# Decode attention with a token mixer on one core: values one pair behind the scores, turns of the keys between the softmax steps

## The chip, the core and the metric

The kernel runs on one core of one Trainium2 chip. The engines that matter here are TensorE (PE, matmuls), VectorE (DVE), ScalarE (ACT), GpSimd (POOL) and SyncE (SP, which issues the DMAs). Each takes its instructions in the order of its own queue; an instruction that waits holds up all behind it. The metric is the device time of one execution in microseconds (us), as a median over runs, less is better.

## What is computed

One decode step for 8 sequences: x (8 tokens of 512 values) plus a grouped-query attention over a cache of 8192 positions, plus a small MLP over the token axis. All is float32. Cut to what matters:

```
x  = A_x;  xn = layernorm(x)
q  = xn @ wq                          # 32 query heads of 128
k, v: caches [B=8, Hkv=8, Sk=8192, Dh=128], four query heads share one key head
p  = softmax(q . k * Dh**-0.5)        # over the 8192 positions
o  = p . v
attention = o @ wo                    # [32*128, 512]
h  = layernorm(xn)
mixer = gelu(h * w1 + b1) . w2 + b2   # 1792 hidden units, one token position
out = x + attention + mixer
```

The keys and values of one (head, sequence) pair are 8192 x 128 floats each, 4 MB (4096 KB) for the keys and 4 MB for the values. There are 8 x 8 = 64 such pairs, and each cache entry is used for four queries only.

## The kernel before

The kernel goes through the 64 pairs i = 0 .. 63 (N_IT), head h = i // 8, sequence b = i % 8. Keys and values are loaded whole, one DMA of 4 MB each (128 partitions, 64 rows of 128 floats in each), into a ring of five buffers named raw (RING, line 36). The loads are listed in advance in `order` (lines 53 to 57: keys 0, values 0, keys 1, values 1, ..., with values 62 put behind keys 63), and `load_next` (67) issues the next one of the list on SP. A load takes the buffer that was taken five loads earlier, and waits on SP until its last reader is done. Three loads are issued ahead of everything, two more after the projection of q, then one in each `qk` and one in each `pv`. The very first keys come in four pieces, the last values in pieces of a half, a quarter and two eighths (line 74).

The steps of one pair:

- `turn(i, a)` (209): DVE transposes a quarter of the keys in place, in 32 x 32 blocks; four turns per pair.
- `qk(i)` (216): 16 matmul calls, 32 matmul instructions, give the scores S of the pair in one PSUM bank; then it issues a load.
- `sm_max` (230, DVE: maximum of a row), `sm_bias` (235: a matmul that spreads the maxima, and a DVE reduction over those of one query head), `sm_exp` (243, ACT: exponential and row sum), `sm_place` (251: a matmul that permutes rows, and a DVE transpose into PT).
- `pv(i)` (261): 16 calls, 32 instructions, multiply PT with the values; it can be called for a part (u0 to u1) of the rows; at its end it issues a load.
- `o_pick(i)` (275, three DVE instructions) takes the wanted blocks out of the product and adds them up; `o_place(i)` (284) adds the pair's columns to MH, a bank that collects one head.

Once a head: `o_sums` (292: row sums and their reciprocal), `o_scale` (299) and `o_project` (303: 32 matmul instructions with wo, then an addition to yacc on DVE), with wo of the head loaded by `load_wo` (83) into a single buffer at b = 2. The mixer of one token runs beside a head: `mx_begin` (315) at b = 0, two or three `mx_step` (324, ACT and POOL) in a pair, `mx_end` (331: 4 matmul calls and an addition). `q_place` (201) writes the queries of the next head into the weights W, at b = 3 to 6.

The schedule is manual: every engine executes in the order in which the code calls the steps. In the main loop (lines 359 to 390) that is, per pair: qk(i), the four softmax steps of i, turn(i + 1, 0), pv(i), mixer, turn(i + 1, quart), o_pick(i), turn(i + 1, 2 * quart), o_place(i), turn(i + 1, 3 * quart). At b = 7 come o_sums, mx_end, o_scale and o_project of the same head. The last two pairs are written out (392 to 416), and the result is stored from yacc (417).

Of the kernel before, what the change touches and what calls it, by code (L numbers as in the profile page):

```python
# [14 lines left out]
B, D, HQ, HKV, SK, DH, F = 8, 512, 32, 8, 8192, 128, 1792  # L15
REP = HQ // HKV
P = 128
NT = SK // P
# [9 lines left out]
N_IT = B * HKV  # L28
# [4 lines left out]
def attn_mixer_kernel(ctx: ExitStack, tc: tile.TileContext, x, kc, vc, wq, wo, w1, b1, w2, b2, out):  # L33
# [12 lines left out]
    def misc():  # L46
        return ps_m.tile([P, 512], F32, name="misc")
# [3 lines left out]
    KR, VR = {}, {}  # L51
    order = []
# [14 lines left out]
    def load_next():  # L67
        if order:
            _, src, to, i = order.pop()
            h, b = divmod(i, B)  # L70
            t = ring.tile([P, NT, DH], F32, name="raw")
            rows = src[b, h].rearrange("(p t) d -> p t d", p=P)
            at = 0
            for n in (NT // 4,) * 4 if to is KR and not i else (NT // 2, NT // 4, NT // 8, NT // 8) if not order else (NT,):
                nc.sync.dma_start(t[:, at:at + n, :], rows[:, at:at + n, :])
                at += n
            to[i] = t
            if not order:
                load_wo(HKV - 1)
# [3 lines left out]
    def load_wo(h):  # L83
        t = one.tile([P, REP, D], F32, name="wo")
        rows = wo[h * REP * DH:(h + 1) * REP * DH, :].rearrange("(r p) n -> p r n", p=P)
        if h < HKV - 1:
            for p in (slice(0, 8), slice(8, P)) if h == HKV - 2 else (slice(0, P),):
                nc.sync.dma_start(t[p], rows[p])
        else:
            for r in range(REP):  # L90
                nc.sync.dma_start(t[:, r, :], rows[:, r, :])
        wos[h] = t
# [116 lines left out]
    def turn(i, a, w=NT // 4):  # L209
        if i < N_IT:  # L210
            t = KR[i][:, a:a + w, :].rearrange("p t d -> p (t d)")
            nc.vector.transpose(t, t)  # L212
# [3 lines left out]
    def qk(i):  # L216
        h, b = divmod(i, B)
        S[i] = ps_s.tile([P, 512], F32, name="s")
        kt = KR.pop(i).rearrange("p (u g) d -> p g u d", g=NG)
        for j in range(NB):  # L220
            for g in range(NG):
                nc.tensor.matmul(S[i][g * Q:(g + 1) * Q, :], W[h % 2][:, b, j, :], kt[:, g, :, j * Q:(j + 1) * Q],  # L222
                                 start=(j == 0), stop=(j == NB - 1))
        load_next()
# [5 lines left out]
    def sm_max(i):  # L230
        mr = work.tile([P, 1], F32, name="mr")
        nc.vector.tensor_reduce(mr, S[i], AX.X, ALU.max)  # L232
        st[i] = mr

    def sm_bias(i):
        m = misc()
        nc.tensor.matmul(m[:, :P], st[i].to_broadcast([P, P]), ident, start=True, stop=True)  # L237
        t = one.tile([P, P], F32, name="sq")
        nb = work.tile([P, 1], F32, name="nb")
        nc.vector.tensor_tensor_reduce(t, m[:, :P], hmask, -SCALE, 3.0e38, ALU.add, ALU.min, nb)  # L240
        st[i] = nb

    def sm_exp(i):
        h, b = divmod(i, B)
        p = t2k.tile([P, 512], F32, name="t2k")
        nc.scalar.activation(p, S.pop(i), AF.Exp, bias=st[i], scale=SCALE, accum_out=LR[h % 2][:, b:b + 1])  # L246
        st[i] = p
# [3 lines left out]
    def sm_place(i):  # L251
        m = misc()
        nc.tensor.matmul(m, perm, st.pop(i), start=True, stop=True)  # L253
        PT[i] = work.tile([P, 512], F32, name="pt")
        nc.vector.transpose(PT[i], m)  # L255
# [5 lines left out]
    def pv(i, u0=0, u1=NU):  # L261
        if u0 == 0:
            O[i] = ps_o.tile([P, 512], F32, name="o")
        for u in range(u0, u1):
            c = u % NB
            nc.tensor.matmul(O[i][c * Q:(c + 1) * Q, :], PT[i][:, u * Q:(u + 1) * Q],  # L266
                             VR[i][:, u * NG:(u + 1) * NG, :].rearrange("p t d -> p (t d)"),
                             start=(u < NB), stop=(u >= NU - NB))
        if u1 == NU:
            del VR[i], PT[i]  # L270
            load_next()
# [3 lines left out]
    def o_pick(i):  # L275
        om = t2k.tile([P, 512], F32, name="t2k")
        nc.vector.tensor_tensor(om.rearrange("p (g d) -> p g d", g=NG), O.pop(i).rearrange("p (g d) -> p g d", g=NG),  # L277
                                dm.unsqueeze(2).to_broadcast([P, NG, DH]), ALU.mult)
        ob = work.tile([P, 256], F32, name="ob")
        nc.vector.tensor_add(ob, om[:, :256], om[:, 256:])  # L280
        nc.vector.tensor_add(ob[:, :DH], ob[:, :DH], ob[:, DH:])  # L281
        OB[i] = ob

    def o_place(i):
        h, b = divmod(i, B)
        if b == 0:
            MH[h] = ps_h.tile([P, 512], F32, name="mh")
        nc.tensor.matmul(MH[h][:, b * REP:(b + 1) * REP], OB.pop(i)[:, :DH], sel, start=True, stop=True)  # L288
# [3 lines left out]
    def o_sums(h):  # L292
        m = misc()
        for r in range(REP):
            nc.tensor.matmul(m[:, r * B:(r + 1) * B], sel[:, r:r + 1].to_broadcast([P, P]), LR[h % 2], start=True, stop=True)
        RD[h] = work.tile([P, REP, B], F32, name="rd")
        nc.vector.reciprocal(RD[h], m[:, :REP * B].rearrange("p (r b) -> p r b", r=REP))

    def o_scale(h):
        nc.vector.tensor_tensor(OTS[h % 2].rearrange("p r (b s) -> p r b s", s=BS)[:, :, :, 0],  # L300
                                MH.pop(h)[:, :REP * B].rearrange("p (b r) -> p r b", r=REP), RD.pop(h), ALU.mult)

    def o_project(h):
        m = misc()
        for r in range(REP):
            for j in range(NB):
                nc.tensor.matmul(m[j * Q:(j + 1) * Q, :D // NB], OTS[h % 2][:, r, :], wos[h][:, r, quarter[j]],
                                 start=(r == 0), stop=(r == REP - 1))
        nc.vector.tensor_add(yacc, m[:, :D // NB], yacc)
# [5 lines left out]
    def mx_begin(b):  # L315
        m = misc()
        nc.tensor.matmul(m, ident[:B, b:b + 1].to_broadcast([B, P]), hn, start=True, stop=True)
        hb = one.tile([P, D], F32, name="hb")
        nc.scalar.copy(hb, m)
        acc = one.tile([P, D], F32, name="macc")  # L320
        nc.gpsimd.memset(acc, 0.0)  # L321
        mx[b] = (hb, acc)

    def mx_step(b, j):
        hb, acc = mx[b]
        g = one.tile([P, D], F32, name="g")
        nc.scalar.activation(g, hb, AF.Gelu_apprx_tanh, bias=b1t[:, j:j + 1], scale=w1t[:, j:j + 1])  # L327
        nc.gpsimd.tensor_scalar(g, g, w2t[:, j:j + 1], 1.0, op0=ALU.mult, op1=ALU.mult)  # L328
        nc.gpsimd.tensor_add(acc, acc, g)  # L329

    def mx_end(b):
        m = misc()
        for j in range(NB):
            nc.tensor.matmul(m[j * Q:(j + 1) * Q, :D // NB], bsel[:, BO - BS * b:BO - BS * b + Q], mx[b][1][:, quarter[j]],  # L334
                             start=True, stop=True)
        nc.vector.tensor_add(yacc, m[:, :D // NB], yacc)
# [18 lines left out]
    quart = NT // 4  # L355

    for i in range(N_IT - 2):
        h, b = divmod(i, B)  # L360
        if i == 0:
            for a in range(4):
                turn(0, a * quart)
        qk(i)
        sm_max(i)
        sm_bias(i)
        sm_exp(i)
        sm_place(i)
        turn(i + 1, 0)
        pv(i)  # L370
        if b == 0:
            mx_begin(h)
        k = 2 if h + 1 < HKV else 3
        for j in range(k * b, min(k * b + k, NF)):
            mx_step(h, j)
        turn(i + 1, quart)
        o_pick(i)
        turn(i + 1, 2 * quart)
        o_place(i)
        if b == B - 1:  # L380
            o_sums(h)
            mx_end(h)
        if b == 2:
            load_wo(h) if h < HKV - 1 else None
        if 3 <= b < 3 + NB and h + 1 < HKV:
            q_place(h + 1, b - 3)
        turn(i + 1, 3 * quart)
        if b == B - 1:
            o_scale(h)
            o_project(h)  # L390

    h = HKV - 1
    i, e = N_IT - 2, N_IT - 1
    qk(i)
    sm_max(i)
    sm_bias(i)
    sm_exp(i)
    sm_place(i)
    for a in range(4):
        turn(e, a * quart)  # L400
    pv(i)
    qk(e)
    o_pick(i)
    sm_max(e)
    sm_bias(e)
    sm_exp(e)
    sm_place(e)
    o_place(i)
    o_sums(h)
    mx_end(h)  # L410
    for u0, u1 in ((0, 8), (8, 12), (12, 14), (14, 16)):
        pv(e, u0, u1)
    o_pick(e)
    o_place(e)
    o_scale(h)
    o_project(h)
    nc.sync.dma_start(out.rearrange("b s (j n) -> j (b s) n", j=NB), yacc[::BS, :])
# [27 lines left out]
```

## Time and profile before

| | |
|---|---|
| median of 3 runs | 1576.01 us (1573.36 to 1576.42) |
| the profiled execution | 1578.8 us, its span from first to last instruction 1576.9 us |
| mean granted TensorE clock | 0.736 of full speed |
| turn of a quarter of the keys (L212, DVE) | 2282 ns, 256 times |
| read from HBM | 553.69 MB |

The profile is of one execution. Its page gives busy times by engine, the span in 40 slices, the DMA queues, the chain of work that ended last (followed back from the last instruction, each step to what released it), and the costliest groups of instructions. L222 is line 222 of the code; PE is the matmul, PEld the load of its weights. In a group's row stand the busy time in us and the mean of one in ns, and after the second bar the engine's idle time just before these instructions and what ended most of it. A row of the table of stages gives, for one stretch of the span, the busy time of each engine with the number of instructions, then the granted clock of TensorE, the mean busy share of the 16 DMA engines, and GB/s. A row of DMA issues ends with the median time from issue to landing in us; a row of waits gives total us, times, and the longest.

### The profile page before, as it was taken

What the parts mean: (1) busy time and instruction counts of PE and PEld (TensorE: products, weight loads), DVE (VectorE), ACT (ScalarE), POOL (GpSimd) and SP (SyncE); (2) the same over time, 40 slices, a digit from 0 to 9 for tenths busy, and PEclk for the clock granted to TensorE, in tenths of its full rate; (3) what the DMA queues carried; (4) which work ended last, traced back from release to release, by engine and by line L of the source; (5) the groups of instructions that cost most, each with busy time, mean ns of one, the idle gap of its engine ahead of it and who ended that gap; (6) DMA issues with size and microseconds to landing.
All of it is one profiled execution on the core that took longest, in us unless ns stands there. A gap on an engine that the chain in (4) does not pass through costs nothing.

```text
span 1576.9 us, 12454 instructions
## 1 busy us (share of the span) xinstructions
PE 928.2 (59%) x5172; PEld 267.0 (17%) x5172; DVE 796.9 (51%) x835; ACT 289.0 (18%) x364; POOL 229.5 (15%) x244
## 2 busy tenths in 40 slices
PE   3565566565565555655656645665656655566556
PEld 3111112111121112111121111211112111121112
DVE  2554645544545546545455445445445455454454
ACT  0121111221121220221202211022211212112110
POOL 1020211211111101111201111011110211113100
PEclk9676677776777767776677776776768777776768
DMA  9999888998888988899889988899888998898880
GB/s 407 430 432 389 353 333 348 370 387 333 346 357 365 370 346 359 345 376 371 334 333 377 382 346 346 342 363 386 360 333 345 374 369 350 333 369 336 336 330 1
DMA packets 24099, 554.51 MB, mean 352 GB/s; under 512 B 2499, under 2 KB 2531, under 8 KB 6891
## 3 DMA queue, kind: packets, MB, share of 16 engines
q1 hardware_dynamic: 23899, 553.67, 86.4%
q8 instruction: 41, 0.67, 0.2%
q14 instruction: 15, 0.12, 0.0%
q0 software_dynamic: 128, 0.02, 0.0%
q10 hardware_dynamic: 16, 0.02, 0.0%
HBM read 553.69 MB, written 0.02 MB: 351 GB/s over the span
## 4 chain that ended last, share of the span: by engine, by line
PE 59%; issue 17%; DVE 15%; ACT 7%; DMA 1%; DVEq 0%; ACTq 0%; SPq 0%
PE o L266 24%; PE s L222 23%; PE misc L253 6%; ACT L246 4%; ACT t2k L246 3%; DVE pt L255 3%; DVE mr L232 3%; DVE t2k L277 3%; DVE raw L212 2%; PE misc L237 2%; DVE ob L280 2%; DMA raw<-in_A_wq_dram 1%; PE mh L288 1%; DVE ob L281 1%; DVE sq L240 1%
## 5 line engine op out<-in xcount | busy, mean ns | idle before, releaser
L212 DVE STREAM_TRANSPOSE raw<-raw 128x2048 f32<-128x2048 f32 x256 | 577.1, 2282 | 0.3
L222 PE MATMUL s<-raw,w 128*32 128x512 f32 x2048 | 359.3, 864 | 254.0 <-issue 221.8
L266 PE MATMUL o<-raw,pt 128*32 128x512 f32 x2048 | 370.3, 890 | 51.0 <-DVE pt L255 51.0
L328 POOL TENSOR_SCALAR g<-g,w2t 128x512 f32<-128x512 f32 x112 | 77.7, 694 | 1071.9 <-ACT g L327 1071.9
L232 DVE TENSOR_REDUCE mr<-s 128x1 f32<-128x512 f32 x64 | 44.3, 691 | 363.4 <-PE s L222 363.4
L246 ACT ACT_TABLE_LOAD x55 | 70.6, 1283 | 799.7 <-DVE nb L240 799.6
L253 PE MATMUL misc<-t2k,perm 128*128 128x512 f32 x128 | 96.2, 840 | 147.5 <-ACT t2k L246 147.5
L222 PEld LDWEIGHTS s<-raw,w 128*32 128x32 f32 x2048 | 90.0, 152 | 466.7 <-issue 433.7
L255 DVE STREAM_TRANSPOSE pt<-misc 128x512 f32<-128x512 f32 x64 | 45.9, 717 | 217.4 <-PE misc L253 217.4
L329 POOL TENSOR_TENSOR macc<-macc,g 128x512 f32<-128x512 f32 x112 | 142.7, 1274 | 9.3
L266 PEld LDWEIGHTS o<-raw,pt 128*32 128x32 f32 x2048 | 82.1, 155 | 351.8 <-issue 227.3
L327 ACT ACTIVATE g<-hb,b1t,w1t 128x512 f32<-128x512 f32 x112 | 91.1, 813 | 127.4 <-POOL macc L329 126.7
L277 DVE TENSOR_TENSOR t2k<-o,dm 128x512 f32<-128x512 f32 x64 | 44.2, 691 | 100.8 <-PE o L266 100.8
L246 ACT ACTIVATE t2k<-s,nb 128x512 f32<-128x512 f32 x64 | 44.0, 687 | 243.6 <-DVE nb L240 243.1
L288 PE MATMUL mh<-sel,ob 128*128 128x4 f32 x128 | 24.5, 262 | 94.5 <-DVE ob L281 94.5
L327 ACT ACT_TABLE_LOAD x54 | 69.3, 1283 | 1.4
L237 PE MATMUL misc<-ident,mr 128*128 128x128 f32 x128 | 31.2, 326 | 52.0 <-DVE mr L232 52.0
L253 PEld LDWEIGHTS misc<-t2k,perm 128*128 128x128 f32 x128 | 21.8, 213 | 159.7 <-ACT t2k L246 159.7
L288 PEld LDWEIGHTS mh<-sel,ob 128*128 128x128 f32 x128 | 19.1, 188 | 154.5 <-DVE ob L281 154.1
L240 DVE CUSTOM_DVE_ANT_0 sq<-misc,hmask 128x128 f32<-128x128 f32 x64 | 18.6, 291 | 44.2 <-PE misc L237 44.2
L237 PEld LDWEIGHTS misc<-ident,mr 128*128 128x128 f32 x128 | 19.0, 187 | 115.9 <-DVE mr L232 115.9
L321 POOL MEMSET macc<- 128x512 f32 x8 | 4.2, 524 | 194.4 <-PE misc L334 194.4
(67 smaller groups left out, 198.2 us busy)
## 6 DMA issues: line engine op xcount, KB each, us to landing
raw<-in_A_v_cache_dram SPq DMA_DIRECT2D x63, 4096.0 KB, 12.8
raw<-in_A_k_cache_dram SPq DMA_DIRECT2D x63, 4096.0 KB, 12.3
raw<-in_A_wq_dram SPq DMA_DIRECT2D x2, 4096.0 KB, 17.1
wo<-in_A_wo_dram SPq DMA_DIRECT2D x6, 1024.0 KB, 14.7
raw<-in_A_k_cache_dram SPq DMA_DIRECT2D x4, 1024.0 KB, 25.4
raw<-in_A_v_cache_dram SPq DMA_DIRECT2D x1, 2048.0 KB
raw<-in_A_v_cache_dram SPq DMA_DIRECT2D x1, 1024.0 KB, 9.4
raw<-in_A_v_cache_dram SPq DMA_DIRECT2D x2, 512.0 KB
```

What stands on the lines that cost most here:

```text
L212: nc.vector.transpose(t, t)
L222: nc.tensor.matmul(S[i][g * Q:(g + 1) * Q, :], W[h % 2][:, b, j, :], kt[:, g, :, j * Q:(j + 1) * Q], start=(j == 0), stop=(j == NB - 1))
L232: nc.vector.tensor_reduce(mr, S[i], AX.X, ALU.max)
L237: nc.tensor.matmul(m[:, :P], st[i].to_broadcast([P, P]), ident, start=True, stop=True)
L246: nc.scalar.activation(p, S.pop(i), AF.Exp, bias=st[i], scale=SCALE, accum_out=LR[h % 2][:, b:b + 1])
L253: nc.tensor.matmul(m, perm, st.pop(i), start=True, stop=True)
L255: nc.vector.transpose(PT[i], m)
L266: nc.tensor.matmul(O[i][c * Q:(c + 1) * Q, :], PT[i][:, u * Q:(u + 1) * Q], VR[i][:, u * NG:(u + 1) * NG, :].rearrange("p t d -> p (t d)") ...
L277: nc.vector.tensor_tensor(om.rearrange("p (g d) -> p g d", g=NG), O.pop(i).rearrange("p (g d) -> p g d", g=NG), dm.unsqueeze(2).to_broadca ...
L327: nc.scalar.activation(g, hb, AF.Gelu_apprx_tanh, bias=b1t[:, j:j + 1], scale=w1t[:, j:j + 1])
L328: nc.gpsimd.tensor_scalar(g, g, w2t[:, j:j + 1], 1.0, op0=ALU.mult, op1=ALU.mult)
L329: nc.gpsimd.tensor_add(acc, acc, g)
```

## The change

The steps keep their code; their order changes. In a slot i, PE now does qk(i), then pv of the pair before, then the matmuls of sm_bias(i), o_place(i - 1) and sm_place(i). On DVE the turns of keys i + 1 stand between: turn 0, sm_max(i), turns 1 and 2, the reduction of sm_bias(i), o_pick(i - 1), turn 3, the transpose of sm_place(i). The calls of load_next stay in qk and pv, and so come in the order qk(i), pv(i - 1). o_sums, o_scale and o_project of a head stand in the first slot of the next one, mx_end at b = 7 (b = 6 in the last head), and the loop runs to pair 62, so that only the last pair is written out. The last keys are loaded in four pieces like the first ones. The number of instructions of each kind stays the same, save for the three DMAs that the pieces add.

```diff
--- before.py
+++ after.py
@@ -71,7 +71,7 @@
             t = ring.tile([P, NT, DH], F32, name="raw")
             rows = src[b, h].rearrange("(p t) d -> p t d", p=P)
             at = 0
-            for n in (NT // 4,) * 4 if to is KR and not i else (NT // 2, NT // 4, NT // 8, NT // 8) if not order else (NT,):
+            for n in (NT // 4,) * 4 if to is KR and i in (0, N_IT - 1) else (NT // 2, NT // 4, NT // 8, NT // 8) if not order else (NT,):
                 nc.sync.dma_start(t[:, at:at + n, :], rows[:, at:at + n, :])
                 at += n
             to[i] = t
@@ -356,62 +356,59 @@
 
 
 
-    for i in range(N_IT - 2):
+    LAST = N_IT - 1
+
+    def slot(i):
+
         h, b = divmod(i, B)
-        if i == 0:
-            for a in range(4):
-                turn(0, a * quart)
         qk(i)
+        turn(i + 1, 0)
         sm_max(i)
+        turn(i + 1, quart)
+        if i:
+            pv(i - 1)
+        turn(i + 1, 2 * quart)
         sm_bias(i)
+        if i:
+            o_pick(i - 1)
+            o_place(i - 1)
         sm_exp(i)
+        turn(i + 1, 3 * quart)
         sm_place(i)
-        turn(i + 1, 0)
-        pv(i)
         if b == 0:
             mx_begin(h)
+            if h:
+                o_sums(h - 1)
+                o_scale(h - 1)
+                o_project(h - 1)
         k = 2 if h + 1 < HKV else 3
         for j in range(k * b, min(k * b + k, NF)):
             mx_step(h, j)
-        turn(i + 1, quart)
-        o_pick(i)
-        turn(i + 1, 2 * quart)
-        o_place(i)
-        if b == B - 1:
-            o_sums(h)
-            mx_end(h)
-        if b == 2:
-            load_wo(h) if h < HKV - 1 else None
+        if b == 2 and h + 1 < HKV:
+            load_wo(h)
         if 3 <= b < 3 + NB and h + 1 < HKV:
             q_place(h + 1, b - 3)
-        turn(i + 1, 3 * quart)
-        if b == B - 1:
-            o_scale(h)
-            o_project(h)
-
+        if b == (B - 1 if h + 1 < HKV else B - 2):
+            mx_end(h)
+
+    for a in range(4):
+        turn(0, a * quart)
+    for i in range(LAST):
+        slot(i)
     h = HKV - 1
-    i, e = N_IT - 2, N_IT - 1
-    qk(i)
-    sm_max(i)
-    sm_bias(i)
-    sm_exp(i)
-    sm_place(i)
-    for a in range(4):
-        turn(e, a * quart)
-    pv(i)
-    qk(e)
-    o_pick(i)
-    sm_max(e)
-    sm_bias(e)
-    sm_exp(e)
-    sm_place(e)
-    o_place(i)
+    qk(LAST)
+    sm_max(LAST)
+    sm_bias(LAST)
+    sm_exp(LAST)
+    sm_place(LAST)
+    pv(LAST - 1)
+    o_pick(LAST - 1)
+    o_place(LAST - 1)
     o_sums(h)
-    mx_end(h)
     for u0, u1 in ((0, 8), (8, 12), (12, 14), (14, 16)):
-        pv(e, u0, u1)
-    o_pick(e)
-    o_place(e)
+        pv(LAST, u0, u1)
+    o_pick(LAST)
+    o_place(LAST)
     o_scale(h)
     o_project(h)
     nc.sync.dma_start(out.rearrange("b s (j n) -> j (b s) n", j=NB), yacc[::BS, :])
```

## The prediction

> **What bounds the kernel now.** I read the page's first lines and its chain of work first, then one pair of that chain, then the table of stages, then the DMA issues and the waits of SP's queue.
>
> ```profile
> span 1576.9 us, 12454 instructions
> PE 928.2 (59%) x5172; PEld 267.0 (17%) x5172; DVE 796.9 (51%) x835; ACT 289.0 (18%) x364; POOL 229.5 (15%) x244
> PE 59%; issue 17%; DVE 15%; ACT 7%; DMA 1%; DVEq 0%; ACTq 0%; SPq 0%
> ```
>
> No engine is busy for more than 59% of the span, and the chain that ended last consists of PE, DVE and ACT in turn, with 1% of DMA. So it is a serial chain, handed from engine to engine. One pair of it, in the view of the chain:
>
> ```profile
> 697.82 5.22 PE s L222 x32
> ...
> 703.81 0.50 PE misc L237 x2
> ...
> 708.25 0.73 DVE pt L255
> 708.98 0.04 issue
> 709.02 6.46 PE o L266 x32
> ...
> 717.41 4.43 issue
> 721.84 5.16 PE s L222 x32
> ```
>
> From scores to scores is 721.84 - 697.82 = 24.0 us: scores 5.2, softmax up to the values' start 6.0, values 6.5, then 6.3 in which DVE picks and still turns the second half of the next keys (shown as "issue"; DVE's turns lie there). Over the run 64 x 24.0 are 1536 of the 1576.9 us. Now the transfers.
>
> ```profile
> core 0: us, PE busy (x) PEld busy (x) DVE busy (x) ACT busy (x) POOL busy (x), PEclk, DMA share, GB/s
> 0.00:40.00 40.00, 15.53 (x292) 12.85 (x292) 10.70 (x39) 3.58 (x7) 5.32 (x13) 1.00 0.97 406
> 40.00:120.00 80.00, 44.81 (x212) 11.63 (x212) 43.49 (x42) 15.50 (x19) 11.81 (x12) 0.70 1.00 431
> ...
> 160.00:1540.00 1380.00, 821.95 (x4390) 228.40 (x4386) 709.99 (x716) 259.27 (x323) 207.97 (x215) 0.73 0.88 354
> ```
>
> ```profile
> DMA packets 24099, 554.51 MB, mean 352 GB/s; under 512 B 2499, under 2 KB 2531, under 8 KB 6891
> ...
> raw<-in_A_k_cache_dram SPq DMA_DIRECT2D x63, 4096.0 KB, 12.3
> ```
>
> ```profile
> 56.62 0.33 SPq L75 DMA_DIRECT2D raw<-in_A_v_cache_dram  x1
> ...
> 703.06 0.33 SPq L75 DMA_DIRECT2D raw<-in_A_v_cache_dram  x1
> ...
> 715.49 0.33 SPq L75 DMA_DIRECT2D raw<-in_A_k_cache_dram  x1
> ```
>
> ```profile
> SPq L75 <- PE o L266: 692.3, 61, 13.0
> ```
>
> While the transfers queued from the start lasted (40 to 120 us) the DMA engines were busy all the time and moved 431 GB/s, beside the same matmuls and turns as later. Afterwards SP waits for PE to free a buffer, and issues one tile at a time: the tile of 703.06 has landed some 12 us later, about when the next is issued at 715.49. The queue runs dry before each issue, and the rate drops to 354. So compute bounds the kernel, and the DMA floor lies close under it: one pair is 2 x 4.194 = 8.389 MB, at 431 GB/s **19.46 us**, against 24.0.
>
> **The change, part by part.** Values one pair later: pv(i-1) no longer waits for the softmax of its own pair; it follows qk(i) on PE, while DVE does the softmax and turns between its steps. What remains serial has to be compared with 19.46. The durations:
>
> ```profile
> L212 DVE STREAM_TRANSPOSE raw<-raw 128x2048 f32<-128x2048 f32 x256 | 577.1, 2282 | 0.3
> L222 PE MATMUL s<-raw,w 128*32 128x512 f32 x2048 | 359.3, 864 | 254.0 <-issue 221.8
> L266 PE MATMUL o<-raw,pt 128*32 128x512 f32 x2048 | 370.3, 890 | 51.0 <-DVE pt L255 51.0
> ...
> L232 DVE TENSOR_REDUCE mr<-s 128x1 f32<-128x512 f32 x64 | 44.3, 691 | 363.4 <-PE s L222 363.4
> ...
> L240 DVE CUSTOM_DVE_ANT_0 sq<-misc,hmask 128x128 f32<-128x128 f32 x64 | 18.6, 291 | 44.2 <-PE misc L237 44.2
> L277 DVE TENSOR_TENSOR t2k<-o,dm 128x512 f32<-128x512 f32 x64 | 44.2, 691 | 100.8 <-PE o L266 100.8
> ...
> L280 DVE TENSOR_TENSOR ob<-t2k 128x256 f32<-128x256 f32 x64 | 28.7, 449 | 2.2
> ...
> L281 DVE TENSOR_TENSOR ob<-ob 128x128 f32<-128x128 f32 x64 | 18.7, 292 | 2.2
> ```
>
> A turn is 2.28, scores 359.3/64 = 5.62, values 370.3/64 = 5.79, the pick 0.69 + 0.45 + 0.29 = 1.43. For the values behind the scores I keep two ends, since PE's clock changes within a burst:
>
> ```profile
> 722.67 0.23 PEld L222 LDWEIGHTS s<-raw,w 128*32 128x32 f32 x4 [0.62 <-issue]
> ...
> 725.49 0.14 PEld L222 LDWEIGHTS s<-raw,w 128*32 128x32 f32 x4 [0.29 <-issue]
> ```
>
> Four matmuls take 0.23 + 0.62 = 0.85 us early in the burst and 0.43 late in it, so 32 take 6.8 at the slow pace and 3.4 at the fast one: pv is 3.4 to 6.8. The Trainium skill ("TensorE: Matmul & The Clock Gate", Part 1) says that the clock is at half until about 3.4 us of activity have passed; the two rows agree with it. By that rule pv right behind qk is at the fast end: the sum below stays, and rival B loses ground.
>
> (1) The chain of one slot, with keys at hand: qk 5.62, pv 3.4 to 6.8, the bias matmul 0.5 (L237 in the chain), the reduction 0.37 with its read-out, the pick 1.43, the last turn 2.28, handovers 0.4: 14.0 to 17.4 us. Softmax's exp, placement and the turn of pt run beside pick and turn. DVE's own load is 796.9/64 = 12.5. All are below 19.46.
>
> (2) The loop through the buffers is the new risk. Five buffers are used in load order; qk(i) now issues the load of keys i+2, and that takes the buffer of values i-1, so it waits on SP for pv(i-1), and the load of values i+2 stands behind it in SP's queue. Both loads of a pair start together, after pv(i-1). Keys i+2 are needed in the next slot by turn(i+2, 0), which stands on DVE in front of sm_max(i+1): while it waits, the maximum, and with it the whole softmax, wait too. From the landing: turn 2.28, maximum 0.69, two turns 4.56, reduction 0.37, pick 1.43, turn 2.28, ten handovers of 0.05: 12.1 to the start of qk(i+2); then 5.62 and 3.4 to 6.8 to the end of pv(i+1), which frees the buffers again, two slots on. That is X = 21.1 to 24.5. With 12.3 from issue to landing on an empty queue the loop is 33.4 to 36.8 in two slots, 16.7 to 18.4 a pair. Below 19.46 again, by 2.1 to 5.5 us in two slots: the second tile of each pair keeps the queue filled until the next issue. So **the DMA becomes the bound** and streams.
>
> (3) Projection one pair later: removed from the end of a head, it now stands on PE between place(i) and the next scores at b = 0.
>
> ```profile
> L307 PE MATMUL misc<-wo,ot 128*32 128x128 f32 x256 | 14.6, 402 | 23.7 <-issue 23.4 <-DVE ot L300 0.3
> ...
> L317 PE MATMUL misc<-hn,ident 8*128 8x512 f32 x16 | 9.0, 639 | 0.0
> L295 PE MATMUL misc<-lr,sel 128*128 128x8 f32 x64 | 8.4, 257 | 0.0
> ```
>
> Per head that is 1.8 + 1.1 + 1.1, and about 0.5 of DVE between them, with handovers some 4.7 us seven times. Hidden by the margin of 5.5; at the other margin, 2.1, it costs 2.6 x 7 = 18 us. I take nothing and keep 18 for the range. The load of wo at b = 2 stays, one more MB in the stream; the mixer's steps and its end are beside it (ACT 18%, POOL 15%).
>
> (4) Last keys in four pieces: they land before DVE is free for them (below); worth nothing, and what cover fails is at most part of one transfer, some 7 us.
>
> **The sum.** By 40 us 40 x 0.406 = 16.2 MB have moved; 538.3 MB are left, at 431 GB/s 1249 us: the stream ends at S = 1289. In the start, scores 0 issue values 2 at 56.62 as now; the next issue comes with pv(0), after 8.4 of DVE (maximum, three turns, reduction), qk(1) and pv(0) itself, at 74 to 77. The eight tiles issued by then, 33.6 MB, last until 40 + 17.4/0.431 = 80: no gap. The end: behind keys 62 come keys 63, values 62, values 63 and 1 MB of wo, 13.6 MB or 31.6 us, so keys 62 land at S - 31.6, qk(62) starts 12.1 later at S - 19.5 and ends at S - 13.9, and after the maximum, three turns, reduction and pick (9.8) qk(63) starts at S - 4.1. The old end gives what follows:
>
> ```profile
> 1555.98 3.64 PE L222 MATMUL s<-raw,w 128*32 128x512 f32 x32 [3.48 <-issue]
> ...
> 1565.23 4.97 PE L266 MATMUL o<-raw,pt 128*32 128x512 f32 x32
> ```
>
> From 1555.98 to 1576.9 are 20.9; qk at its mean adds 2.0, values 62 and their pick, which had been done by then, 5.1 (the middle of 3.4 and 6.8) + 1.4. So 29.4 from S - 4.1: span 1289 + 25.3 = 1314. The profiled execution of before took 1578.8 for a span of 1576.9, so 1.9 more: 1316. The median of the runs, 1576.01, is 2.8 below it; in that proportion 1313.
>
> **Rivals.** (A) is this forecast; a rate half a per cent higher and a tail of 20 give 1302, and if the 406 of the first 40 us (with the start in it) were the rate, 1391; I take 431, the row with the same work beside it. **(B) The buffer loop decides.** If X is 28 rather than 24.5 the pair takes (12.3 + 28)/2 = 20.15, times 62 some 43 us more: 1356; at X = 30 it is 21.15 and 1418; at 31.7 the queue runs dry each slot by about what the issue costs, and it is 1470. For it: the margin is thin, handovers are estimates, PE's clock is uncertain. Against: even all matmuls at the slow pace (qk 6.8) leave X at 25.7. **(C) The memory gives no more than 354 GB/s for long**, and the 431 were a burst: then after 120 us, with 50.7 MB moved, the other 503.8 MB take 1423 us, and with the tail it is about 1567, 0.6% faster, give or take the tail. Against it: in the middle each tile is issued only when the one before has landed, so the empty queue explains the low rate. The Trainium skill ("DMA: Bandwidth & Descriptors", Specifications) gives about 358 GB/s as one core's limit on HBM; by that all 554.51 MB take 1549 us and the whole with its tail 1574, no change; the 80 us at 431 speak against it as a hard limit. **(D) Slower:** the turn at the head of DVE's queue. Were X above 2 x 24.0 - 12.3 = 35.7, a pair would take longer than 24. That wants 11 us more in X; its place would be the four turns, which now always run beside a transfer and beside matmuls that read the same buffers: from 5.1 us a turn on it decides, and at 5.5 a pair is 24.9 and the time about 1647. Against it, from 40 to 120 us, with the DMA always busy:
>
> ```profile
> L212 DVE STREAM_TRANSPOSE raw<-raw 128x2048 f32<-128x2048 f32 x16 | 35.8, 2278 | 0.0
> ```
>
> A turn took 2.28 there too. That the change would not do what it says has no case of its own: the orders of PE, DVE and SP are those of the code.
>
> **Chances and range.** A 0.70, B 0.20, C 0.05, D 0.05. The range, 1296 to 1375, holds A down to a rate of some 415 GB/s (1362) and the near part of B, up to X = 28.6. A change of 0.2% (3 us) is about what a measurement of this kernel can tell from none. A and B are faster; of C, whose time hangs on the tail and on the exact cap, I count 0.03 as faster and 0.02 as same; D is slower: faster 0.93, same 0.02, slower 0.05.
>
> **What would show it.** Right: in the middle stretch a DMA share near 1.00 and about 430 GB/s; issues of SP in pairs, one keys and one values at the end of L266; a time to landing some us above 12 for keys and above 22 for values; DVE waiting at L212 for a DMA; a pair of 19.5; PE's values at 3.4 to 6.8 directly behind the scores; the last transfers ending about 25 us before the end. B: a DMA share of 0.9 to 0.97, with L212 waiting and dips at b = 0. C: share 1.00 at a low rate. D: L212 far over 2.28. I would be wrong if a wait that I have not listed stands in DVE's queue, since everything there waits in line.

## The result, and the profile after

The changed kernel takes 1326.09 us (median of 4 runs, 1324.89 to 1326.68) against 1575.06 us for the kernel before (4 runs): ratio 0.842, 95% interval 0.840 to 0.843. The forecast was 1313 us with a range of 1296 to 1375. The profiled execution took 1324.89 us, its span 1323.1 us.

The page of the changed kernel: span, busy time, the DMA engines' share in 40 slices (tenths) with the rate below it, and the chain that ended last.

```profile
span 1323.1 us, 12383 instructions
PE 790.6 (60%) x5172; PEld 260.9 (20%) x5172; DVE 806.1 (61%) x835; ACT 289.0 (22%) x364; POOL 230.9 (17%) x244
...
DMA  9999999999999999999999999999999999999993
GB/s 397 437 432 427 429 427 434 432 427 429 432 430 430 427 432 431 431 424 432 432 431 427 429 430 427 434 422 429 432 429 428 433 342 429 435 430 420 432 423 126
...
DMA 53%; PE 22%; DVE 16%; issue 4%; ACT 4%; SPq 0%; ACTq 0%; DVEq 0%
```

The chain of before had 1% of DMA; this one has 53%. The engines do the same work (PE's busy time fell, since more of its matmuls ran at the fast pace), in 254 us less. The DMA digits are 9 from the first slice to the last but one. The table of stages of the changed kernel, columns as before:

```profile
40.00:120.00 80.00, 42.83 (x244) 11.97 (x244) 50.97 (x43) 15.90 (x20) 11.80 (x12) 0.72 1.00 429
...
160.00:1270.00 1110.00, 676.70 (x4256) 218.88 (x4260) 691.42 (x693) 256.38 (x319) 205.76 (x211) 0.75 1.00 427
...
1300.00:1324.00 24.00, 13.81 (x132) 5.17 (x124) 5.39 (x13) 0.78 (x2) 0.00 (x0) 0.93 0.05 20
```

The middle stretch, which had 0.88 and 354 GB/s, has 1.00 and 427. That is most of the gain: the 488 MB that took 1380 us at 354 GB/s take 1144 us at 427 GB/s, which is 236 of the 254 us. Groups of instructions, and below them the waits of SP's queue (total us, times, longest):

```profile
L212 DVE STREAM_TRANSPOSE raw<-raw 128x2048 f32<-128x2048 f32 x256 | 582.1, 2294 | 380.1 <-DMA raw<-in_A_k_cache_dram 380.1
L222 PE MATMUL s<-raw,w 128*32 128x512 f32 x2048 | 322.2, 785 | 17.0 <-issue 11.8
...
L266 PE MATMUL o<-raw,pt 128*32 128x512 f32 x2048 | 231.0, 592 | 0.0
```

```profile
SPq L75 <- DVE raw L212: 605.8, 62, 19.6
SPq L75 <- PE s L222: 393.3, 62, 12.0
SPq L75 <- PE o L266: 184.5, 61, 3.1
```

The wait has moved: DVE, which waited for no transfer before, waits 380.1 us at the first turn of a slot for keys, 6.1 us a slot. It is the wait of an engine that has room. A turn still takes 2.29 us. The values take 231.0/64 = 3.61 us a pair instead of 5.79 and wait for nothing.

### The profile page after: what moved, and what is told of

Its sections match the earlier page's. It is cut to its first block, busy times and chain, and to the rows that moved or that the text cites. A ratio compares the mean times of both kernels' runs of the same rounds, so it can differ in the third digit from the quotient of the medians.

```text
span 1323.1 us, 12383 instructions
## 1 busy us (share of the span) xinstructions
PE 790.6 (60%) x5172; PEld 260.9 (20%) x5172; DVE 806.1 (61%) x835; ACT 289.0 (22%) x364; POOL 230.9 (17%) x244
## 4 chain that ended last, share of the span: by engine, by line
DMA 53%; PE 22%; DVE 16%; issue 4%; ACT 4%; SPq 0%; ACTq 0%; DVEq 0%
DMA raw<-in_A_k_cache_dram 53%; DVE raw L212 13%; PE s L222 13%; PE misc L253 5%; ACT L246 2%; DVE mr L232 2%; ACT t2k L246 1%; PE misc L317 1%; PE misc L307 1%; PE misc L295 1%; PE o L266 1%; DVE t2k L277 1%; DVE sq L240 0%; PE mh L288 0%; DVE ob L280 0%
## 5 line engine op out<-in xcount | busy, mean ns | idle before, releaser
L212 DVE STREAM_TRANSPOSE raw<-raw 128x2048 f32<-128x2048 f32 x256 | 582.1, 2294 | 380.1 <-DMA raw<-in_A_k_cache_dram 380.1
L222 PE MATMUL s<-raw,w 128*32 128x512 f32 x2048 | 322.2, 785 | 17.0 <-issue 11.8
L266 PE MATMUL o<-raw,pt 128*32 128x512 f32 x2048 | 231.0, 592 | 0.0
L288 PE MATMUL mh<-sel,ob 128*128 128x4 f32 x128 | 35.6, 349 | 322.1 <-DVE ob L281 322.1
L253 PE MATMUL misc<-t2k,perm 128*128 128x512 f32 x128 | 125.4, 1080 | 15.6 <-ACT t2k L246 15.6
L222 PEld LDWEIGHTS s<-raw,w 128*32 128x32 f32 x2048 | 76.8, 143 | 275.5 <-issue 262.8
L288 PEld LDWEIGHTS mh<-sel,ob 128*128 128x128 f32 x128 | 30.0, 291 | 336.6 <-DVE ob L281 336.6
L266 PEld LDWEIGHTS o<-raw,pt 128*32 128x32 f32 x2048 | 62.2, 110 | 157.8 <-issue 157.8
L205 DVE COPY w<-qt 32x128 f32<-32x128 f32 x64 | 37.1, 617 | 0.7
L253 PEld LDWEIGHTS misc<-t2k,perm 128*128 128x128 f32 x128 | 30.8, 299 | 20.0 <-ACT t2k L246 20.0
L280 DVE TENSOR_TENSOR ob<-t2k 128x256 f32<-128x256 f32 x64 | 27.2, 425 | 2.2
## 6 DMA issues: line engine op xcount, KB each, us to landing
raw<-in_A_v_cache_dram SPq DMA_DIRECT2D x63, 4096.0 KB, 28.9
raw<-in_A_k_cache_dram SPq DMA_DIRECT2D x62, 4096.0 KB, 22.6
```

## Experiments

The control, the changed kernel once more on the chip of three others, took 1324.91 us (ratio to the kernel before 0.840, 0.839 to 0.842). Ratios below are to the kernel before on the same chip.

### Each of the two parts alone

Turns behind the softmax again, values one pair later:

```diff
         qk(i)
-        turn(i + 1, 0)
         sm_max(i)
-        turn(i + 1, quart)
...
-        turn(i + 1, 2 * quart)
...
-        turn(i + 1, 3 * quart)
         sm_place(i)
+        for a in range(4):
+            turn(i + 1, a * quart)
```

> The changed kernel, but the four turns of the next keys stand behind the softmax steps of the slot again (values stay one pair later). If the gain needs both parts, the slot is serial again: scores 5.2, values 3.6, bias matmul and reduction 1.0, exp with its table 2.1, placement 2.1, turn of pt 0.7, four turns 9.1: about 24 us a pair and 1560 to 1600 us, as before. If the later values alone gave the gain: 1326 to 1400.

Measured: 1584.26 us, ratio 1.005 (1.004 to 1.007). The later values alone gain nothing, although their matmuls run as fast here as in the changed kernel (597 ns on average, against 592), so faster values by themselves are not the gain. In its chain of work, the scores of two pairs one after the other:

```profile
715.89 6.29 PE s L222 x32
...
730.76 9.61 issue
740.38 5.99 PE s L222 x32
```

From 715.89 to 740.38 are 24.5 us. PE does the values at once behind the scores, with the maximum beside them, but then the reduction, the exponential, the placement and four turns on DVE (the 9.61 us of "issue" before the next scores) are in line. What the values left has been filled by the turns.

Turns between the softmax steps, values in their own slot:

```diff
         turn(i + 1, quart)
-        if i:
-            pv(i - 1)
         turn(i + 1, 2 * quart)
         sm_bias(i)
-        if i:
-            o_pick(i - 1)
-            o_place(i - 1)
         sm_exp(i)
         turn(i + 1, 3 * quart)
         sm_place(i)
+        pv(i)
+        o_pick(i)
+        o_place(i)
...
-    pv(LAST - 1)
-    o_pick(LAST - 1)
-    o_place(LAST - 1)
```

> The changed kernel, but values follow the softmax of their own pair; the turns stay between the softmax steps. If both parts are needed: scores 5.5, maximum 0.8, two turns 4.5, reduction 0.4, exp 2.1, placement 2.1, pt 0.8, values 5 to 6, pick and placement 1.9 are serial, about 23.5 us a pair and 1500 to 1570 us. If the turns between the steps alone gave the gain: 1326 to 1400.

Measured: 1476.91 us, ratio 0.937 (0.935 to 0.939): 23 us below the times that were expected if both parts are needed, a miss, and still far from 1326. The timeline of this kernel (start, length), two pairs:

```profile
716.77 3.64 PE L222 MATMUL s<-raw,w 128*32 128x512 f32 x32
...
730.86 4.96 PE L266 MATMUL o<-raw,pt 128*32 128x512 f32 x32 [0.81 <-DVE pt L255]
...
737.74 3.64 PE L222 MATMUL s<-raw,w 128*32 128x512 f32 x32
```

This pair takes 737.74 - 716.77 = 21.0 us; from the first scores (49.35 us) to the last (1450.81 us) the mean is 22.2. The expectation had the scores at 5.5; here they follow the values of the pair before and run at the fast pace, 3.64. Values, pick, scores and softmax are in line, and no turn is, except the two in front of the reduction. Alone the parts give +8 and -99 us; together -249. Each takes one piece out of the serial chain, and the chain falls under the 19.5 us of the transfers only when both are out.

### The loop through the buffers

The prediction let both loads of a slot wait for the values. The changed kernel does something else. Its timeline over a slot (SPq: an issue on SP's queue):

```profile
708.83 2.31 DVE L212 STREAM_TRANSPOSE raw<-raw 128x2048 f32<-128x2048 f32 x1 [1.16 <-DMA raw<-in_A_k_cache_dram]
...
728.25 2.31 DVE L212 STREAM_TRANSPOSE raw<-raw 128x2048 f32<-128x2048 f32 x1 [6.68 <-DMA raw<-in_A_k_cache_dram]
...
739.95 5.55 PE L222 MATMUL s<-raw,w 128*32 128x512 f32 x32
...
745.32 3.61 PE L266 MATMUL o<-raw,pt 128*32 128x512 f32 x32
745.57 0.33 SPq L75 DMA_DIRECT2D raw<-in_A_k_cache_dram  x1
747.69 2.31 DVE L212 STREAM_TRANSPOSE raw<-raw 128x2048 f32<-128x2048 f32 x1 [6.92 <-DMA raw<-in_A_k_cache_dram]
749.00 0.33 SPq L75 DMA_DIRECT2D raw<-in_A_v_cache_dram  x1
```

Keys are issued at 745.57, when the scores end (739.95 + 5.55), and values at 749.00, when the values of the pair before end. So the keys take the buffer of the keys that the scores just finished, and not that of the values. The last of the three rows of SP's waits above agrees: a load of values waits 184.5/61 = 3.0 us, the time from the end of the scores to the end of the values. To see whether the waits that the prediction assumed would have cost anything, I ran a kernel with them: a small matmul behind the values reads the keys once more, so that their buffer, too, comes free only there, and both loads are issued behind it.

```diff
 (qk)
-        kt = KR.pop(i).rearrange("p (u g) d -> p g u d", g=NG)
+        kt = (KR[i] if i else KR.pop(i)).rearrange("p (u g) d -> p g u d", g=NG)
...
-        load_next()
+        if i == 0:
+            load_next()
 (pv)
             del VR[i], PT[i]
+            if i + 1 in KR:
+                m = misc()
+                nc.tensor.matmul(m[:Q, :Q], W[0][:, 0, 0, :], KR.pop(i + 1)[:, 0, :Q], start=True, stop=True)
             load_next()
+            load_next()
```

> The changed kernel with the buffers in the rotation that the prediction assumed: a small matmul behind the values reads the keys once more, so that both loads of a slot wait for the end of the values. If the DMA is the bound and the loop has room, as the prediction's step 2 says with the measured 5.0 and 3.6 us (33.3 us of loop in 38.9): within 1% of 1326 us (1322 to 1340). If the loop through the buffers is tight (rival B): 1350 to 1420.

Measured: 1328.88 us, ratio 0.843 (0.841 to 0.845), no difference that the intervals show. Both loads now wait for that matmul, and the stream stays full (waits of SP's queue, and the middle stretch):

```profile
SPq L75 <- PE misc L274: 1160.7, 61, 26.1
```

```profile
160.00:1270.00 1110.00, 673.36 (x4334) 229.78 (x4338) 691.54 (x693) 256.30 (x319) 204.15 (x210) 0.75 1.00 425
```

So the loop has room even in the longer form, as step 2 of the prediction had worked out, though for an order of buffers that the changed kernel doesn't have.

### How much room compute has

The last turn of each slot three times (three transposes are one), 4.56 us more:

```diff
-        turn(i + 1, 3 * quart)
+        for _ in range(3):
+            turn(i + 1, 3 * quart)
```

> The changed kernel with the last turn of each slot done three times (three transposes equal one), 4.56 us more on DVE and in the chain of a slot. DVE waits 380.1 us in 62 waits, 6.1 a slot, for keys: if the DMA is the bound, that takes it up and the time stays within 1% (1322 to 1340). If compute or the loop binds, the pair grows by 1.2 to 4.6 us: 1400 to 1610.

Measured: 1347.58 us, ratio 0.855 (0.853 to 0.857), 22 us more than the changed kernel; a miss by 8 us. Its rows: the turns with the waits before them, and one pair, from scores to scores.

```profile
L212 DVE STREAM_TRANSPOSE raw<-raw 128x2048 f32<-128x2048 f32 x382 | 873.5, 2300 | 82.0 <-DMA raw<-in_A_k_cache_dram 77.5
```

```profile
732.00 5.99 PE L222 MATMUL s<-raw,w 128*32 128x512 f32 x32 [5.56 <-DVE raw L212]
...
737.82 3.61 PE L266 MATMUL o<-raw,pt 128*32 128x512 f32 x32
...
738.07 0.69 DVE L232 TENSOR_REDUCE mr<-s 128x1 f32<-128x512 f32 x1 [3.33 <-PE s L222]
738.67 4.50 DVE L212 STREAM_TRANSPOSE raw<-raw 128x2048 f32<-128x2048 f32 x2
741.35 0.49 PE L237 MATMUL misc<-ident,mr 128*128 128x128 f32 x2
...
743.09 0.25 DVE L240 CUSTOM_DVE_ANT_0 sq<-misc,hmask 128x128 f32<-128x128 f32 x1
...
744.67 7.00 DVE L212 STREAM_TRANSPOSE raw<-raw 128x2048 f32<-128x2048 f32 x3
...
751.77 1.08 PE L222 MATMUL s<-raw,w 128*32 128x512 f32 x4 [5.08 <-issue]
```

291 us were added to DVE, 303 of its 380 us of waiting went, and 22 us showed. This pair, in which no instruction waits for a transfer, takes 751.77 - 732.00 = 19.77 us: the chain of a slot is now about as long as the transfers take, and in 42 slots DVE still waits for keys. Without the addition it is 19.77 - 4.56 = 15.2 us. The rows also show which way that chain goes: scores, maximum, two turns, reduction, pick, last turns, all on DVE after the scores. The values and the bias matmul are done (741.4 and 741.8) before the two turns are (743.2), so they are not in it. Where the time went can be read from the two profiles, whose spans differ by 23.2 us: the scores of pair 62 start 13.1 us later (1295.55 against 1282.45), 0.2 us a pair; from there to the last scores it is 4.8 us more, since nothing covers the addition in the last keys; and behind the last scores 5.3 us more, where more of PE's matmuls run at the slow pace (the last scores take 6.26 us against 5.12).

The other way round, half of the values' bytes: of values 2 to 62 only the first half is loaded, and used twice; the instructions of the engines stay the same in number and size.

```diff
-                nc.sync.dma_start(t[:, at:at + n, :], rows[:, at:at + n, :])
+                m = n // 2 if to is VR and 2 <= i < N_IT - 1 else n
+                nc.sync.dma_start(t[:, at:at + m, :], rows[:, at:at + m, :])
 (pv)
+            v = u % (NU // 2) if 2 <= i < N_IT - 1 else u
...
-                             VR[i][:, u * NG:(u + 1) * NG, :].rearrange("p t d -> p (t d)"),
+                             VR[i][:, v * NG:(v + 1) * NG, :].rearrange("p t d -> p (t d)"),
```

> The changed kernel, but of values 2 to 62 only the first half is loaded and used twice, so the output isn't the reference's; the instructions of PE, DVE, ACT and POOL stay the same in number and size. The stream of a pair falls from 8.39 to 6.29 MB, 14.7 us at 428 GB/s. If the DMA is the bound and the chain of a slot is 15.2 us (19.77 with three turns more in place of one, less 4.56), with some 4.7 more in one slot of eight: 15.8 us a pair, 1040 to 1090 us. If compute or the loop stood close behind the 19.5 us: 1200 to 1326.

Measured: 1093.76 us, ratio 0.694 (0.691 to 0.696), 4 us above what was expected. Its middle stretch:

```profile
160.00:1050.00 890.00, 645.62 (x4202) 208.06 (x4201) 677.89 (x684) 251.64 (x313) 202.39 (x207) 0.81 0.95 399
```

With a quarter of the bytes gone the kernel is 232 us faster with the same compute, and the DMA share is still 0.95. That the transfers are the bound of the changed kernel is shown by this and by the turns that could be added nearly free.

### A dip in the stream, the end of the kernel, and a faster version

In the row of rates above one slice has 342 GB/s. Closer, in the changed kernel, the stretches around it, and the issue that comes before:

```profile
1060.00:1070.00 10.00, 7.05 (x58) 1.87 (x50) 3.51 (x3) 0.81 (x1) 1.97 (x2) 0.94 1.00 428
1070.00:1080.00 10.00, 4.41 (x16) 1.51 (x20) 8.57 (x11) 4.16 (x5) 1.57 (x2) 0.58 1.00 225
1080.00:1090.00 10.00, 7.01 (x60) 1.67 (x52) 0.00 (x0) 0.81 (x1) 2.46 (x3) 0.91 1.03 340
```

```profile
1047.22 0.76 SPq L88 DMA_DIRECT2D wo<-in_A_wo_dram  x2
```

These are the two DMAs of wo for head 6, of 8 and 120 partitions (line 87). The share is full, the rate half.

```diff
-            for p in (slice(0, 8), slice(8, P)) if h == HKV - 2 else (slice(0, P),):
+            for p in (slice(0, P),):
```

> The changed kernel, with the wo of head 6 loaded by one DMA like the others instead of 8 and 120 partitions. The changed kernel moves 225 and 340 GB/s in 1070 to 1090 us, just behind those two DMAs, with DMA share 1.00. If the split makes this, about 3 MB at 431 GB/s come back: 5 to 8 us less than the control (0.4 to 0.6%). If something else makes it: no change.

Measured: 1318.70 us, 6.2 less than the control; ratio 0.836 (0.835 to 0.838). In that kernel the dip is gone:

```profile
1070.00:1080.00 10.00, 4.33 (x14) 1.43 (x17) 8.88 (x11) 4.16 (x5) 1.26 (x2) 0.54 1.01 419
1080.00:1090.00 10.00, 6.79 (x60) 1.64 (x52) 1.06 (x1) 0.81 (x1) 2.76 (x3) 0.95 0.99 426
```

The end of the kernel: there keys 62 set off the chain that ends last. They can land one transfer earlier if values 61 come behind them, and values have room, since they are used one pair later.

```diff
-        order.append((2 * i + (1 if i < N_IT - 2 else 2.5), vc, VR, i))
+        order.append((2 * i + 2.5, vc, VR, i))
```

> The changed kernel with values i listed behind keys i+1 in the order of loads, all through. In the middle nothing changes, since the stream stays as it is. At the end keys 62 land 9.7 us earlier, and the chain that ended last starts there: 4 to 9 us less than the control if the end of the kernel hangs on those keys; no change if it hangs on the last values.

Measured: 1317.09 us, 7.8 less than the control; ratio 0.835 (0.833 to 0.837). The first turn of keys 62 starts at 1261.90 us in its trace, against 1270.76 in the changed kernel, 8.9 us earlier.

> Both edits together, values later in the order of loads and wo of head 6 in one DMA: 10 to 16 us less than the control if the two are independent, some 1310 to 1316 us.

Measured: 1308.76 us, 16.1 less than the control; ratio 0.830 (0.828 to 0.832). The two add up, 6.2 + 7.8 = 14.0 against 16.1, and this version is faster than both kernels.

The four pieces of the last keys, first in the changed kernel, then in this version; the edit is the same:

```diff
-            for n in (NT // 4,) * 4 if to is KR and i in (0, N_IT - 1) else (NT // 2, NT // 4, NT // 8, NT // 8) if not order else (NT,):
+            for n in (NT // 4,) * 4 if to is KR and not i else (NT // 2, NT // 4, NT // 8, NT // 8) if not order else (NT,):
```

> The changed kernel with the last keys in one DMA again. In its trace the first turn of keys 63 follows the transpose of pt at once (1283.19 us) and waits for no transfer, so the pieces should be worth nothing, as the prediction's step 4 says: 1323 to 1329 us. If they matter: up to 7 us more.

Measured: 1326.13 us, ratio 0.842 (0.840 to 0.843): nothing.

> The kernel with values later in the order of loads and wo in one DMA, but the last keys in one DMA. There keys 63 are wanted at 1266.7 us, 17 us earlier than in the changed kernel, before the last quarter can have landed. If the four pieces pay only where the end waits for these keys: 3 to 8 us more than with pieces, 1312 to 1317. If never: 1307 to 1311.

Measured: 1314.93 us, ratio 0.835 (0.833 to 0.836), against 0.830 with the pieces: 6 us. The first turn of keys 63 in the changed kernel, in the version with both edits, and in that without the pieces:

```profile
1283.19 2.27 DVE L212 STREAM_TRANSPOSE raw<-raw 128x2048 f32<-128x2048 f32 x1
```

```profile
1266.65 2.27 DVE L212 STREAM_TRANSPOSE raw<-raw 128x2048 f32<-128x2048 f32 x1
```

```profile
1273.65 2.31 DVE L212 STREAM_TRANSPOSE raw<-raw 128x2048 f32<-128x2048 f32 x1 [6.91 <-DMA raw<-in_A_k_cache_dram]
```

In the first DVE comes to these keys after they have landed, so their pieces bring nothing. In the second it comes 17 us earlier and finds the first piece there; without pieces it waits 6.91 us for the whole.

## Why the prediction held, and where it was off

**The bound.** Right. The serial chain of 24.0 us fell under the transfers, and the kernel runs at the rate that the stretch from 40 to 120 us had shown: 427 GB/s over 1110 us, where the prediction took 431.

**The chain of a slot.** Forecast 14.0 to 17.4 us; through the added turns it comes out at 15.2, but it goes another way than the sum did. The sum went along PE, over values and bias matmul; with the values at 3.61 that makes 14.2. The rows above show the longer way along DVE: with the prediction's own figures scores 5.62, maximum 0.69, two turns 4.56, reduction 0.37, pick 1.43, last turn 2.28 and handovers 0.4 are 15.4. Step 1 left out the maximum and two turns, which step 2 has, so that the 15.2 lie inside the forecast is in part luck. The values behind the scores came out at the fast end, 3.61; what the Trainium skill says of the clock ("TensorE: Matmul & The Clock Gate", Part 1) fits that row: with the scores ahead of them, all values' matmuls run at 592 ns, where the mean was 890. The scores in front of them stayed at the slow pace for longer in some pairs than the 3.4 us that the prediction took from the Trainium skill (in the one at 721.03 the weights are loaded every 0.85 us until 726.16, and every 0.43 us from 726.90 on), so the row shows that the scores were long enough, and not that figure.

**The loop.** Its conclusion held and its premise was wrong. "Five buffers are used in load order", so that keys wait for the values of the pair before: the issues at 745.57 and 749.00 show that keys wait for the scores, and only values for values. From the landing of keys to the next scores are 739.95 - 728.25 = 11.7 us (forecast 12.1). With the kernel's own order of buffers the loop ends with the scores: 11.7 + 5.55 and 12.3 from issue to landing are 29.6 in two slots of 19.5, so there was more room than the prediction thought. The kernel with the assumed waits costs nothing either. One reading of the code fits both traces, and could have been made before the run: in the order of the calls, a load takes the one buffer whose last reader stands just ahead of it. Before, that made values follow keys and keys follow values (703.06 at the end of the scores, 715.49 at the end of the values), which is the same as the buffer of five loads earlier. In the changed kernel qk(i) is called ahead of pv(i - 1), so its load finds only the buffer of keys i given up, and keys follow keys. Two signs that the prediction named came out differently: the issues of a slot are 3.4 us apart, keys at the end of the scores, and keys take 22.6 us to land (18.9 in the kernel with the assumed waits), not some us above 12; values take 28.9, where it said above 22.

**The projection.** Right in being hidden. At the slot after a head's end the wait at the first turn is 1.16 us instead of 6.7 to 6.9 (708.83 against 728.25 and 747.69): the added work eats 5.5 us of DVE's room, and 18 us that were kept for the range weren't needed.

**The last keys.** Right: worth nothing here (0.842 in both). They are worth 6 us where the order of loads makes the end wait for them.

**The sum.** Neither of these errors reached the time, since both sums stay under 19.46 with the right terms too; the forecast is bytes over a rate, plus the two ends. It is 13 us short: 9 in the span (1314 against 1323.1), and 4 in the step from the profiled execution to the median, taken as -2.8 us from before, while here the median is 1.2 us above it; a step of that size lies within the scatter of the runs of before (1573.36 to 1576.42 us, the profiled one 1578.8). In the span the mis-sized term is S, the end of the stream, forecast at 1289. Two DMAs of wo that the prediction counted as bytes at 431 GB/s cost 6.2 us more than bytes, as their repair shows. The rest of the stream ran at 429, not 431, GB/s (middle of the kernel with wo in one DMA), which over 538 MB is 6 us. The end was forecast at 25.3 us behind the stream. The last transfers end near 1301 (the stretch from 1300 on moves 0.5 MB), 22 us before the end of the span; that term was 3 us too long.

**The rivals.** B fell: room in the loop and in the slot. C fell: 427 GB/s held for 1110 us. The 358 GB/s that the Trainium skill ("DMA: Bandwidth & Descriptors", Specifications) gives as one core's limit on HBM did not bind here, with one core at work. D fell: a turn takes 2.29 us beside a stream that never pauses, against 2.28.

## What to carry to other kernels

If a kernel has one stretch in which the transfers are full and another in which the queue runs dry between issues, the rate of the first is what the second can reach, and everything serial per tile has to come under that time before any of it pays; here one part alone gave nothing and the other 99 us, and both gave 249. Once transfers are the bound, small things in the stream show: a DMA cut in an odd way, or the order of the last loads, which together gave another 16 us. And a piece of an edit that is worth nothing where it is put may be worth something after the next one.

## What the runs showed of the hardware

A DMA of 1 MB to 128 partitions, cut into 8 and 120 partitions, held the stream at 225 and 340 GB/s for 20 us with all DMA engines counted as busy, and cost 6.2 us; in one DMA the same 20 us show 419 and 426 GB/s. That the cut does it is shown; how it does was not tried. And the rate of the stream was nearly the same with more and less work beside it: 431 GB/s in the early stretch of before with DVE busy for 54% of the time, 427 over 1110 us with 62%, and 424 over the same stretch with the last turn done three times and DVE busy for 84%. No run here has the stream without compute.
